# Another transfer model in the simulation that orders an attention and MoE kernel, new wanted times, and a column of ones written ahead of v's load

## The chip, the cores and the metric

The kernel runs on one core of one Trainium2 chip. The metric is the device time of one execution in microseconds (us), median of the runs shown.

## The reference

Queries are averaged in pairs along the sequence, attention is computed for 32 heads (4 batches of 8, 1152 keys, 576 pooled queries, 64 wide), and the result goes as 2304 tokens of 512 through one layer of products (512 to 1024 and back) with SoLU and a norm between them:

```python
q_pool = q.reshape(B, H, S // 2, 2, D).mean(axis=3)
scores = 1 / sqrt(D) * q_pool @ k.T
attn = exp(scores - max);  attn = attn / (sum + 1e-9)
x = (attn @ v)                      # to B * S/2 tokens of H * D = 512
h = x @ w_in                        # 512 -> 1024
e = exp(h - max);  solu = h * e / (sum(e) + 1e-9)
ln = (solu - mean) / sqrt(var + 1e-6) * g_ln
out = ln @ w_out                    # 1024 -> 512
```

## The kernel before

**Tiles and stages.** Heads are prepared in pairs: q, k and v are loaded, transposed on TensorE and split into a high and a low part, so that products keep float32 accuracy (`prep_k`, `prep_q2`, `add_v`). The low and high halves of k reach their places by four transfers from buffer to buffer (`k_put`), the two halves of q by four more (`q_beside`), and a second copy of k's high half by one (`k_again`). For each head `maxima` multiplies q by k once to find the row maxima. `scores` then takes nine steps a head (one for every 128 keys, 288 in all): products on TensorE, exponentials on ScalarE (once to float32 and once to float16, or float32 alone, from which VectorE casts where `use_dve` says so), the rest e - float16(e) on GpSimd (`rest`), and the products with v in groups of steps (`values`, grouped by `GR`). The first pair (18 steps) keeps float32 values in the buffer `vx`: there v lies in rows of 65 elements, the 65th a one that sums the weights. The weights of the two layers come in as 16 raw parts of 512 KB (`weight_part`), each turned into float32 by two ScalarE operations, one on GpSimd, two on VectorE, and split by one more on ScalarE and VectorE. Tokens go through the layers in 18 tiles (`tokens`). The last five need the last batch and run after the last step.

**Order.** Nothing here is put in order by hand. Every operation is given to a `Plan` with its engine, its length, what it reads and writes, and a wanted time `at`, counted in steps of the scores. `Plan.run` simulates the engines: of the operations that are ready it takes the one with the earliest wanted time on each engine, none that is wanted later than the current step plus a window (`win`), and it fills TensorE's idle time at the start with throw-away transposes (line 1374). The order in which the simulation starts operations is the order in which they are issued, engine by engine, and no engine passes over an instruction that waits. All transfers go by one queue, SP's. In the simulation a transfer takes SP for some time a call, enters one common line of transfers, and has an end that its readers wait for:

```python
if e == "SP":
    busy[e] = t + 670 * o.calls
    dma = max(dma, t + 1100) + length
    o.end = dma + 1000
```

**Names that the steps below use.** `KP` (line 21) holds all wanted times: `W` when the weight parts come, `M` when the tokens come, `P` when a pair's k, q and v are loaded and prepared, `N` and `N1` when the maxima start, `OF` other distances, `CD` which steps VectorE casts, `TP` up to which step the two halves of a step share one exponential of 576, `TX` up to which step a second pair of PSUM banks is used, `VM` which engines scale v of each pair, `GG` the head from which values are grouped in three instead of five groups. `v32` makes the buffer `vx`, `load_v32` loads the first pair's v into it, one head a call, and `add_v` sets the column of ones there by a memset on GpSimd (line 813).

Of the kernel before, what the change touches and what calls it, by code (L numbers as in the profile page):

```python
# [17 lines left out]
ALU = mybir.AluOpType  # L18
AXX = mybir.AxisListType.X

KP = {'W': [2, 4, 5], 'step': 0.5, 'M': [77, 15.3, 7.49], 'TX': 113, 'TP': 72, 'win': 5.01, 'P': [22.92, 18.98, 13.92, 23.51, 26.08, 30.44], 'N': [13, 7], 'AV': 3.97, 'CD': [73, 13], 'VM': 'BCCCCABCBABBCCAC', 'AH': 8, 'OF': [5.14, 2.07, 10.29, 1.04, 2.66], 'N1': 10.46, 'warm': 1, 'ws': 1.3, 'GR': 1, 'GG': 12, 'b_eh': 6, 'b_w1': 4, 'V0': -53.76, 'VF': 1, 'QD': [0, 1], 'L0': 0.97, 'F': 18}
FIRST = KP.get("L0", 0.3)


# [15 lines left out]
class Plan:  # L40
# [61 lines left out]
    def run(self):  # L102
# [16 lines left out]
        busy = dict.fromkeys(ready, 0)  # L119
# [65 lines left out]
        while events:  # L185
            t, what, _, arg = heapq.heappop(events)
            if what == 0:
                o, done = arg, done + 1
                for b in o.uses:
                    count[b] -= 1  # L190
                    for i in where[b]:
                        last[i][o.engine] = o
                    if not count[b]:
                        for i in where[b]:
                            held[i] = None
                        for e in ready:
                            push(t, 1, e)
                for m in after[o]:
                    e = m.engine
                    hop = self.HOP[o.engine][e] + (self.LOAD[m.kind] if e == "PE" != o.engine else 0)  # L200
                    if o.engine == e and not m.deps[o]:
                        hop = 0
                    m.ok_at = max(m.ok_at, t + hop)
                    m.left -= 1
                    if not m.left:
                        ready[e].append(m)
                        push(m.ok_at, 1, e)
                continue
            e = arg
            if busy[e] > t:  # L210
                continue
            best = None
            limit = 1e9 if not todo else now_mark + (self.window if todo < len(marks) else FIRST)
            for o in ready[e]:
                if o.at > limit or o.ok_at > t or (best is not None and (o.at, o.n) >= (best.at, best.n)):
                    continue
                g = buffers(o)
                if g is None:
                    continue
                s = could(o, g)  # L220
                if s > t:
                    push(s, 1, e)
                    continue
                best, got = o, g
            if best is None:
                if e == "PE" and self.warm and t > KP.get("ws", 2.5) * 1000 and todo > self.warm_until:
                    i = next((i for i in range(8) if held.get(i) is None), None)
                    if i is not None:
                        extra.append((t, lambda i=i: self.warm(i)))
                        busy[e] = t + (110 if t > self.COLD else 216)  # L230
                        push(busy[e], 1, e)
                continue
            o = best
            ready[e].remove(o)
            for b, c in got.items():
                where[b] = c
                before[b] = [x for i in c for x in last[i].values()]
                for i in c:
                    held[i] = b
                    last[i] = {}  # L240
                if b[0] in self.banks:
                    self.bank[b] = c
                else:
                    turn[self.tags[b[0]][0]] += 1
                head[b[0]] += 1
            for d in (*o.deps, *(x for b in o.uses for x in before.get(b, ()))):
                known[e][d.engine] = max(known[e][d.engine], d.rank)
            o.start, o.rank = t, ranks[e]
            ranks[e] += 1
            length = o.length  # L250
            if e == "PE":
                length += self.SWITCH if kind == "half" != o.kind else 0
                kind = o.kind
                length *= 1 if t > self.COLD else 2
            if e == "SP":
                busy[e] = t + 670 * o.calls
                dma = max(dma, t + 1100) + length
                o.end = dma + 1000
            else:
                busy[e] = o.end = t + length  # L260
            if o.mark is not None:
                todo -= 1
                if o.mark > now_mark or not todo:
                    now_mark = o.mark
            for x in ready:
                push(t, 1, x)
            push(o.end, 0, o)
            push(busy[e], 1, e)
# [25 lines left out]
    return 1.885 * n + 148  # L294


def DMA(n, fast=1):
    return n / (360 if fast else 180)


@with_exitstack
def attention_solu_moe(
# [10 lines left out]
    nc = tc.nc  # L313
# [146 lines left out]
    def weight_part(n, at, src, i, f, dst_h, dst_l, dst):  # L460
# [15 lines left out]
            else:  # L476
                nc.sync.dma_start(out=raw, in_=src[rows, c])

        add("SP", DMA(4096 * 128), at - 3, fetch, [], [("raw", n)])
        if wide:  # L480


# [59 lines left out]
    def pair(P, at_k, at_q, at_v, loads):  # L542
# [23 lines left out]
        def load_v32(i):  # L566
            nc.sync.dma_start(out=v32(P)[:, i, :, 0:D], in_=v[b, h0 + i].rearrange("(p j) d -> p j d", j=NJ))
# [7 lines left out]
        kb = 128 * NJ * D * 4  # L575
        KT = ("vx", 0, "kt") if P == FN == 1 else ("kt", P)
        if P:
            add("SP", DMA(2 * kb, 0), at_lk, load_k, [("vx", 0, 0, "one")] if P == FN == 1 else [], [KT], calls=2)
        else:
            add("SP", DMA(kb), at_lk, lambda: load_k0(0), [], [("kt", 0, 0)])  # L580
        add("SP", DMA(2 * kb), at_lq, load_q, [], [("qt", P, i) for i in range(3)])
        if not P:
            add("SP", DMA(kb), at_lk + 0.1, lambda: load_k0(1), [], [("kt", 0, 1)])
        if P < FN:
            for i in range(2):
                add("SP", DMA(kb, 0), at_lv + i / 10, lambda i=i: load_v32(i), [], [("vx", 0, P % 2, "v", i)])
        else:
            add("SP", DMA(2 * kb), at_lv, load_v, [], [("vt", P)])

# [43 lines left out]
        def k_put(h, lo):  # L633
            g = 2 * P + h
            if ("w1", g) not in tl:
                new(("w1", g), [128, S], FR)
            src = flat(tl["klo" if lo else "khi", P][D * h:D * h + D])
            dst = tl["w1", g][D * lo:D * lo + D, :]
            nc.sync.dma_start(out=dst.bitcast(F32), in_=src.bitcast(F32))
# [21 lines left out]
        def prep_k(i, at):  # L661
            ps, hi, lo = ("kps", (P, i)), ("khi", P, i), ("klo", P, i)
            add("PE", TR(3), at, lambda: k_tr(i), [KT], [ps], also=[hi, lo], kind="whole")
            add("ACT", ACT(PW), at, lambda: k_hi(i), [ps], [hi])
            add("DVE", DVE(PW) + 4, at, lambda: k_lo(i), [ps, hi], [lo])
            if i == 2:
                for h in range(2):
                    for l in range(2):
                        add("SP", DMA(64 * S * 4), at + 4 * h + 0.5, lambda h=h, l=l: k_put(h, l),
                            [("klo" if l else "khi", P)], [("w1", 2 * P + h, l)])  # L670

        def q_tr(i):
# [63 lines left out]
        def prep_q2(at):  # L736
            for i in range(2):
                ps, a = ("qps", (P, i)), at + 2 * i
                add("PE", TR(3 - i), a, lambda i=i: q_tr2(i), [("qt", P, 0)], [ps], also=[("q1", P), ("q2", P)], kind="whole")
                for odd in range(2):  # L740
                    n, o = ((384, 384), (256, 128))[i][odd], a + odd / 10
                    hi, lo = ("q1", P, i, odd), ("q2", P, 2 * i + odd)
                    add("ACT", ACT(n), o, lambda i=i, odd=odd: q_hi2(i, odd), [ps], [hi])
                    add("DVE", DVE(n), o, lambda i=i, odd=odd: q_lo2(i, odd), [ps, hi], [lo])
            for odd in range(2):
                add("SP", DMA(64 * 4 * 576, 0), at + 3, lambda odd=odd: q_beside(odd),
                    [("q1", P, i, odd) for i in range(2)], [("q1", P, 2, odd)], calls=2)
            add("SP", DMA(128 * 256, 0), at + 3, q_half, [("q1", P, 1, 0)], [("zq", P)], calls=2)

        for i in range(3):  # L750
            prep_k(i, at_k[i]) if P else prep_k0(i, 0, at_k[i], [])
# [57 lines left out]

        def add_v(after):  # L810
            if P < FN:
                if P < 2:
                    add("POOL", 160, -13, lambda: nc.gpsimd.memset(v32(P)[:, :, :, D:D + 1], 1.0),
                        [], [("vx", 0, P % 2, "one")])
                return
            V, S, H_ = ("vt", P), ("vs", P, 1), ("vhi", P, 0)
            add("ACT", ACT(2 * SQ, 1, 1), at_v, v_sum, [V, *after], [("am", P, 0), ("vlo", P, 0)])
# [135 lines left out]
    def scores(g, at):  # L953
# [8 lines left out]
        def k_again():  # L962
            nc.sync.dma_start(out=w2[g % 2][0:D, :].bitcast(F32), in_=tl["w1", g][0:D, :].bitcast(F32))

        add("SP", DMA(64 * S * 4), at - OF[0], k_again, [("w1", g)], [("w2", g)])

        def product(j, f):
            if NJ * g + j < TP:
# [345 lines left out]
    with tc.manual_schedule():  # L1314
# [46 lines left out]
        t = MS  # L1361
# [44 lines left out]
```

## Time and profile before

| | |
|---|---|
| median of 3 runs | 729.42 us (728.45 to 732.87) |
| the profiled execution | 732.07 us |
| its span, first to last instruction | 730.3 us |
| mean granted TensorE clock | 0.978 |
| TensorE, matmuls busy | 686.0 us, 94% of the span |
| ScalarE / VectorE / GpSimd busy | 534.7 / 506.5 / 486.4 us |
| the chain that ended last, by engine | TensorE 66%, VectorE 12%, ScalarE 8%, GpSimd 5%, transfers 3%, issue 5% |

The span is that of the profiled execution, and 1.8 us lie around it. A matmul's end is modelled, so a TensorE that counts as busy may still be held up. Idle time of an engine that doesn't set the end costs nothing. PE is TensorE's matmuls, PEld its weight loads, DVE VectorE, ACT ScalarE, POOL GpSimd, and SPq the transfers that SP issues.

### The profile page before, as it was taken

To read this page: it belongs to the slowest core of one execution; us is meant where nothing else is said; L and a number is where in the kernel's file an instruction comes from. 1 tells how busy PE (TensorE), PEld (TensorE's weight loads), DVE (VectorE), ACT (ScalarE), POOL (GpSimd) and SP (SyncE) were. 2 spreads that over 40 slices of the span, in tenths; PEclk is the share of its full clock that TensorE was granted. 3 is DMA by queue.
4 is the path that set the end of the run, shared out by engine and by line. 5 is a ranking of instruction groups with operands and counts; after the bars stand their busy time and mean duration, and the time that the engine had idled before them with its cause. 6 is when DMAs were issued, how large, how long until landed. Compare 5 with 4: busy or idle time off the path is not lost.

```text
span 730.3 us, 18791 instructions
## 1 busy us (share of the span) xinstructions
PE 686.0 (94%) x7048; PEld 598.7 (82%) x7048; DVE 506.5 (69%) x1221; ACT 534.7 (73%) x1327; POOL 486.4 (67%) x635
## 2 busy tenths in 40 slices
PE   7999787999989999999998999899999999999996
PEld 7989676777877888887887898788888898887885
DVE  5896786787887677877858684858586867425542
ACT  2656797989797687888778796778788877773432
POOL 1233796989788678697868677686967777681111
PEclk8999898999999999999999999999999999999999
DMA  8585566674453352536253434425445310000011
GB/s 206 156 210 152 152 161 160 180 182 101 123 120 96 90 135 53 133 88 163 41 128 98 113 84 113 101 65 135 101 102 130 91 42 18 17 16 22 15 30 29
DMA packets 78086, 75.79 MB, mean 104 GB/s; under 512 B 61108, under 2 KB 61228, under 8 KB 77996
## 3 DMA queue, kind: packets, MB, share of 16 engines
q1 hardware_dynamic: 77996, 74.60, 42.0%
q8 instruction: 55, 0.90, 0.5%
q14 instruction: 35, 0.29, 0.1%
HBM read 37.22 MB, written 4.72 MB: 57 GB/s over the span
## 4 chain that ended last, share of the span: by engine, by line
PE 66%; DVE 12%; ACT 8%; issue 5%; POOL 5%; DMA 3%; SPq 1%; ACTq 0%; DVEq 0%; POOLq 0%
PE bank L419 60%; DVE mx L859 4%; POOL eh L1005 3%; PE bank L1224 2%; ACT e L982 2%; PE bank L624 1%; ACT eh L988 1%; DVE q L422 1%; DVE eh L995 1%; DMA raw<-in_moe_w_in_dram 1%; PE bank L1374 1%; ACT e L988 1%; ACT q L718 1%; ACT eh L982 1%; DMA q<-q 1%
## 5 line engine op out<-in xcount | busy, mean ns | idle before, releaser
L1005 POOL TENSOR_TENSOR eh<-e,eh 128x64 f16<-128x64 f32 (+1 forms) x486 | 381.2, 809 | 123.7 <-ACT e L982 29.1
L859 DVE TENSOR_REDUCE mx<-bank 128x1 f32<-128x384 f32 x420 | 220.5, 550 | 79.4 <-PE bank L419 76.5
L419 PE MATMUL bank<-q,w 128*128 128x288 f32 (+1 forms) x1152 | 242.6, 314 | 11.3 <-ACT e L982 7.9
L419 PEld LDWEIGHTS bank<-q,w 128*128 128x128 f32 (+1 forms) x1152 | 188.2, 192 | 37.1 <-ACT e L982 17.8
L982 ACT ACTIVATE eh<-bank 128x288 f16<-128x288 f32 x376 | 159.1, 425 | 59.4 <-PE bank L419 57.2
L982 ACT ACTIVATE e<-bank 128x288 f32<-128x288 f32 x432 | 180.8, 427 | 22.5 <-POOL eh L1005 10.8
L419 PE MATMUL bank<-w,q 128*128 128x384 f32 x390 | 133.9, 371 | 12.9 <-DVE q L422 5.4
L419 PEld LDWEIGHTS <-eh 128*128 128x128 f16 x3834 | 126.6, 99 | 18.4 <-issue 11.2
L419 PE MATMUL bank<-vhi,eh 128*128 128x65 f16 x2484 | 136.2, 196 | 1.8 <-POOL eh L1005 0.9
L419 PE MATMUL bank<-vlo,eh 128*128 128x64 f16 x1350 | 133.1, 194 | 0.0
L419 PEld LDWEIGHTS bank<-w,q 128*128 128x128 f32 x390 | 72.8, 194 | 26.8 <-DVE mx L859 7.8
L1207 POOL TENSOR_TENSOR st<-st 128x1 f32<-128x1 f32 x54 | 23.4, 432 | 57.0 <-ACT junk L1194 53.9
L988 ACT ACTIVATE eh<-bank 128x576 f16<-128x576 f32 (+1 forms) x72 | 47.6, 667 | 12.6 <-PE bank L419 12.0
L493 POOL TENSOR_TENSOR up<-up,un 128x512 f32<-128x512 f32 x16 | 20.9, 1309 | 32.2 <-ACT un L486 14.9
L1155 DVE TENSOR_REDUCE st<-bank 128x1 f32<-128x512 f32 x36 | 24.7, 686 | 24.4 <-PE bank L419 24.3
L422 DVE TENSOR_TENSOR q<-bank,q 64x384 fp32r<-64x384 f32 (+2 forms) x63 | 28.8, 458 | 16.4 <-ACT q L718 13.4
L419 PE MATMUL bank<-woh,lh 128*128 128x512 f32 x104 | 34.3, 416 | 3.2 <-DVE e L1174 3.1
L988 ACT ACTIVATE e<-bank 128x576 f32<-128x576 f32 x54 | 36.1, 672 | 0.2 <-POOL eh L1005 0.2
L419 PE MATMUL bank<-wih,xl 128*128 128x512 f32 x104 | 33.8, 409 | 0.0
L419 PE MATMUL bank<-wol,lh 128*128 128x512 f32 x104 | 32.9, 399 | 0.0
L419 PE MATMUL bank<-wih,xh 128*128 128x512 f32 x104 | 32.7, 403 | 0.0
L419 PE MATMUL bank<-wil,xh 128*128 128x512 f32 x104 | 32.7, 398 | 0.0
(134 smaller groups left out, 1064.9 us busy)
## 6 DMA issues: line engine op xcount, KB each, us to landing
qt<-in_q_dram SPq DMA_DIRECT2D x16, 576.0 KB
w<-w SPq DMA_DIRECT2D x32, 288.0 KB
kt<-in_k_dram SPq DMA_DIRECT2D x30, 288.0 KB
vt<-in_v_dram SPq DMA_DIRECT2D x15, 576.0 KB
w<-khi SPq DMA_DIRECT2D x30, 288.0 KB
w<-klo SPq DMA_DIRECT2D x30, 288.0 KB
out_dram<-o SPq DMA_DIRECT2D x36, 128.0 KB
raw<-in_moe_w_in_dram SPq DMA_DIRECT2D x8, 511.6 KB
```

The lines of the kernel that those rows point to most:

```text
L419: nc.tensor.matmul(out=o, lhsT=a, rhs=b, start=first, stop=last, skip_group_check=True)
L422: nc.vector.tensor_tensor(out=o, in0=a, in1=b, op=ALU.subtract)
L493: nc.gpsimd.tensor_tensor(out=up, in0=up, in1=tl["un", n].bitcast(F32), op=ALU.subtract)
L624: nc.tensor.transpose(ps[:, c, :], tl["kt", P][:, 3 * i + c].rearrange("p h d -> p (h d)"), ident)
L718: nc.scalar.copy(out=tl["q1", P][r, :, t, :], in_=ps)
L859: nc.vector.tensor_reduce(out=tl["mx", g][:, m, c:c + 1], in_=tl["nps", (g, m, c)], op=ALU.max, axis=AXX)
L982: nc.scalar.activation(out=tl[name, (g, j)][:, f * HALF:(f + 1) * HALF], in_=tl[tn(j, f), (g, j, f)], func=ACTF.Exp, scale=ESC,)
L988: nc.scalar.activation(out=new((name, (g, j)), [128, SQ * 4 // mybir.dt.size(dtype)], dtype)[:, 0:SQ].rearrange("p (f i) -> p f i", f=2), ...
L1005: nc.gpsimd.tensor_tensor(out=e[:, o:o + c.stop - c.start], in0=e32[:, c], in1=e[:, c], op=ALU.subtract)
L1155: nc.vector.tensor_reduce(out=st(f), in_=tl[H_[f]], op=ALU.max, axis=AXX)
L1207: nc.gpsimd.tensor_tensor(out=st(o), in0=st(a), in1=nhalf if b is None else st(b), op=op)
L1224: nc.tensor.transpose(ps[:, c, :], tl[E][:, o:o + 128], ident)
```

## The change

The simulation's transfers change in three places: an SP call takes 640 ns instead of 670, a transfer enters the line after 1200 ns instead of 1100, and its end is 2000 ns (`DL`) instead of 1000 after its last byte. Its bytes per ns are no longer 360 or 180 but 300, 260, 250 or 200 by kind. The wanted times in `KP` are other ones. The memset of the ones is put ahead of v's load: it is wanted at -40 instead of -13, and the load names the column as something that it reads, so that it is simulated and issued after the memset. Which instructions exist changes only by `CD`, `TP`, `VM` and `GG`.

```diff
-KP = {'W': [2, 4, 5], 'step': 0.5, 'M': [77, 15.3, 7.49], 'TX': 113, 'TP': 72, 'win': 5.01, 'P': [22.92, 18.98, 13.92, 23.51, 26.08, 30.44], 'N': [13, 7], 'AV': 3.97, 'CD': [73, 13], 'VM': 'BCCCCABCBABBCCAC', 'AH': 8, 'OF': [5.14, 2.07, 10.29, 1.04, 2.66], 'N1': 10.46, 'warm': 1, 'ws': 1.3, 'GR': 1, 'GG': 12, 'b_eh': 6, 'b_w1': 4, 'V0': -53.76, 'VF': 1, 'QD': [0, 1], 'L0': 0.97, 'F': 18}
+KP = {'W': [2.0, 3.15, 5], 'step': 0.46, 'M': [77, 16.35, 7.49], 'TX': 114, 'TP': 76, 'win': 4.7, 'P': [22.28, 18.98, 13.92, 24.38, 26.08, 32.99], 'N': [12.95, 7], 'AV': 4.32, 'CD': [65, 16], 'VM': 'BCCCCABCBAACCCAC', 'AH': 8, 'OF': [6.79, 2.07, 11.42, 1.2, 1.48], 'N1': 9.3, 'warm': 1, 'ws': 1.3, 'GR': 1, 'GG': 6, 'b_eh': 6, 'b_w1': 4, 'V0': -60.99, 'VF': 1, 'QD': [0, 1], 'L0': 0.97, 'F': 18, 'DL': 2000}
...
-                busy[e] = t + 670 * o.calls
-                dma = max(dma, t + 1100) + length
-                o.end = dma + 1000
+                busy[e] = t + 640 * o.calls
+                dma = max(dma, t + 1200) + length
+                o.end = dma + KP.get("DL", 1000)
...
-def DMA(n, fast=1):
-    return n / (360 if fast else 180)
+def DMA(n, rate=300):
+    return n / rate
...
-        add("SP", DMA(4096 * 128), at - 3, fetch, [], [("raw", n)])
+        add("SP", DMA(4096 * 128, 250), at - 3, fetch, [], [("raw", n)])
...
-        add("SP", DMA(2 * kb), at_lq, load_q, [], [("qt", P, i) for i in range(3)])
+        add("SP", DMA(2 * kb, 260), at_lq, load_q, [], [("qt", P, i) for i in range(3)])
...
         if P < FN:
+            if P < 2:
+                add("POOL", 160, -40, lambda: nc.gpsimd.memset(v32(P)[:, :, :, D:D + 1], 1.0),
+                    [], [("vx", 0, P % 2, "one")])
             for i in range(2):
-                add("SP", DMA(kb, 0), at_lv + i / 10, lambda i=i: load_v32(i), [], [("vx", 0, P % 2, "v", i)])
+                add("SP", DMA(kb, 200), at_lv + i / 10, lambda i=i: load_v32(i), [("vx", 0, P % 2, "one")],
+                    [("vx", 0, P % 2, "v", i)])
...
-                        add("SP", DMA(64 * S * 4), at + 4 * h + 0.5, lambda h=h, l=l: k_put(h, l),
+                        add("SP", DMA(64 * S * 4, 200), at + 4 * h + 0.5, lambda h=h, l=l: k_put(h, l),
...
-                add("SP", DMA(64 * 4 * 576, 0), at + 3, lambda odd=odd: q_beside(odd),
+                add("SP", DMA(64 * 4 * 576, 200), at + 3, lambda odd=odd: q_beside(odd),
...
         def add_v(after):
             if P < FN:
-                if P < 2:
-                    add("POOL", 160, -13, lambda: nc.gpsimd.memset(v32(P)[:, :, :, D:D + 1], 1.0),
-                        [], [("vx", 0, P % 2, "one")])
                 return
...
-        add("SP", DMA(64 * S * 4), at - OF[0], k_again, [("w1", g)], [("w2", g)])
+        add("SP", DMA(64 * S * 4, 200), at - OF[0], k_again, [("w1", g)], [("w2", g)])
```

The loads of k, the second half of the q copies and the 16 KB copies (`q_half`) go to 200 as well, which is left out here.

## Rows read from the trace of the kernel before

**Rows 1.** The page: busy us, share of the span, instructions.
```profile
PE 686.0 (94%) x7048; PEld 598.7 (82%) x7048; DVE 506.5 (69%) x1221; ACT 534.7 (73%) x1327; POOL 486.4 (67%) x635
```

**Rows 2.** The waits: us in total, times, longest us.
```profile
PEld L419 <- issue: 11.2, 43, 0.7
...
PE bank L419 <- ACT e L982: 7.9, 16, 1.8
```

**Rows 3.** The timeline's start: us, duration, what, [idle before, releaser].
```profile
0.72 0.39 SPq L561 DMA_DIRECT2D qt<-in_q_dram  x1
...
2.10 6.14 SPq L567 DMA_DIRECT2D vx<-in_v_dram  x2
...
4.74 0.63 DVE L593 TENSOR_TENSOR qt<-qt 128x192 f32<-128x192 f32 x2 [1.50 <-DMA qt<-in_q_dram]
4.79 1.28 ACT L597 ACT_TABLE_LOAD   x1 [4.79 <-DMA qt<-in_q_dram]
...
7.53 0.13 POOL L813 MEMSET vx<- 128x18 f32 x1 [5.37 <-DMA vx<-in_v_dram]
7.60 0.59 POOL L593 TENSOR_TENSOR qt<-qt 128x192 f32<-128x192 f32 x1
8.22 0.35 ACT L597 COPY qt<-qt 128x192 f32<-128x192 f32 x1 [2.15 <-POOL qt L593]
...
8.48 1.22 ACT L649 CAST w<-bank 64x384 fp32r<-64x384 f32 x3
...
9.58 0.90 PE L675 MATMUL bank<-ident,qt 128*128 128x128 f32 x3 [2.80 <-DVE w L422]
```

**Rows 4.** The chain of waits from 60 to 80 us: start, us, what.
```profile
65.43 1.40 SPq L639
...
66.87 7.26 DMA raw<-in_moe_w_in_dram
```

**Rows 5.** The timeline from 60 to 80 us.
```profile
74.16 0.75 ACT L486 ACTIVATE up<-raw,ebias 128x512 int32<-128x512 int8 x1 [5.08 <-DMA raw<-in_moe_w_in_dram]
...
75.34 0.64 ACT L718 CAST q<-bank 64x256 fp32r<-64x256 f32 x2
...
76.79 1.28 PE L419 MATMUL bank<-w,q 128*128 128x384 f32 x2 [4.07 <-DVE q L422]
```

**Rows 6.** The timeline from 96 to 124 us.
```profile
106.02 3.25 SPq L728 DMA_DIRECT2D q<-q  x4
...
113.69 0.66 PE L419 MATMUL bank<-w,q 128*128 128x384 f32 x1 [4.42 <-DMA q<-q]
```

**Rows 7.** The timeline around 457 us.
```profile
456.54 0.59 ACT L1230 CAST lh<-bank 128x512 fp32r<-128x512 f32 x1 [2.26 <-DMA out_dram<-o]
...
457.80 0.54 PE L419 MATMUL bank<-q,w 128*128 128x288 f32 x2 [1.79 <-ACT e L982]
```

**Rows 8.** Busy time by window: length, PE, PEld, DVE, ACT, POOL; PEclk, DMA share, GB/s.
```profile
30.00:40.00 10.00, 10.00 (x83) 9.72 (x82) 9.06 (x20) 8.20 (x16) 1.83 (x2) 1.00 0.87 234
...
40.00:50.00 10.00, 9.54 (x56) 7.24 (x56) 9.83 (x22) 4.00 (x7) 5.62 (x4) 1.00 1.06 209
75.00:85.00 10.00, 7.99 (x53) 6.61 (x53) 7.69 (x16) 8.11 (x15) 8.13 (x6) 0.66 0.33 94
110.00:120.00 10.00, 6.31 (x89) 6.00 (x90) 5.02 (x14) 4.98 (x9) 4.10 (x4) 0.66 0.75 192
140.00:150.00 10.00, 8.05 (x86) 6.56 (x82) 8.51 (x22) 9.78 (x19) 9.53 (x9) 0.91 0.98 238
455.00:465.00 10.00, 8.01 (x72) 6.65 (x71) 6.16 (x19) 5.17 (x14) 4.28 (x6) 0.83 0.39 94
```

**Rows 9.** Groups by line and shape: busy us, mean ns of one, idle before.
```profile
L982 ACT ACTIVATE e<-bank 128x288 f32<-128x288 f32 x432 | 180.8, 427 | 22.5 <-POOL eh L1005 10.8 <-PE bank L419 10.7
...
L988 ACT ACTIVATE e<-bank 128x576 f32<-128x576 f32 x54 | 36.1, 672 | 0.2 <-POOL eh L1005 0.2
...
L995 DVE CAST eh<-e 128x576 f16<-128x576 f32 x28 | 17.4, 623 | 14.9 <-ACT e L982 14.6
...
L497 DVE TENSOR_SCALAR bank<-raw 128x512 int32<-128x512 int32 x16 | 10.9, 683 | 0.1
```

More of the change, by code (lines that the diff above doesn't have):

```diff
@@ L577, in pair @@
         if P:
-            add("SP", DMA(2 * kb, 0), at_lk, load_k, [("vx", 0, 0, "one")] if P == FN == 1 else [], [KT], calls=2)
+            add("SP", DMA(2 * kb, 200), at_lk, load_k, [("vx", 0, 0, "one")] if P == FN == 1 else [], [KT], calls=2)
         else:
             add("SP", DMA(kb), at_lk, lambda: load_k0(0), [], [("kt", 0, 0)])
-        add("SP", DMA(2 * kb), at_lq, load_q, [], [("qt", P, i) for i in range(3)])
+        add("SP", DMA(2 * kb, 260), at_lq, load_q, [], [("qt", P, i) for i in range(3)])
         if not P:
@@ L745, in prep_q2 @@
             for odd in range(2):
-                add("SP", DMA(64 * 4 * 576, 0), at + 3, lambda odd=odd: q_beside(odd),
+                add("SP", DMA(64 * 4 * 576, 200), at + 3, lambda odd=odd: q_beside(odd),
                     [("q1", P, i, odd) for i in range(2)], [("q1", P, 2, odd)], calls=2)
-            add("SP", DMA(128 * 256, 0), at + 3, q_half, [("q1", P, 1, 0)], [("zq", P)], calls=2)
+            add("SP", DMA(128 * 256, 200), at + 3, q_half, [("q1", P, 1, 0)], [("zq", P)], calls=2)
         for i in range(3):
```

## The prediction

> **What bounds the kernel now.** I read the page first. TensorE's matmuls are busy for 686.0 us, far ahead of the other engines [rows 1], so 44 us (730.3 less 686.0) is all the idle time that an order can give back, with whatever the clock costs on top. I then went through TensorE's timeline for every idle stretch of 0.45 us or more: 24 of them, 28.8 us together. Four end on something that a transfer held up, and they make 13.1 us: 2.80 at 9.58 us [rows 3], 4.07 at 76.79 us [rows 5], 4.42 at 113.69 us [rows 6] and 1.79 at 457.80 us [rows 7]. The other twenty share 15.8 us, mostly below a microsecond each.
>
> Last came the windows, for what the clock and the other engines do there. The clock reads 0.66 in the ten microseconds round the second stall, 0.66 round the third and 0.83 round the fourth: between its levels of 1.2 and 2.4 GHz, after TensorE had stood still. From 40 to 50 us VectorE is busy for 9.83 of 10 us, and TensorE, which counts as busy for 9.54, gets only 56 matmuls through; in the ten microseconds before there were 83 [rows 8]. So that stretch is VectorE's, whatever the busy share says.
>
> **The column of ones.** Its memset stands behind v's load in the program, and both touch the interleaved rows of `vx`. The row shows what comes of it: the memset sits idle on GpSimd for 5.37 us until the load is in, runs for 0.13 us, and only then may GpSimd add the last third of q, which ScalarE copies at 8.22 us and behind which its first cast of k stands at 8.48 us. The second call of v's load is stuck behind the memset too (two calls take SP 6.14 us) [rows 3].
>
> Put first, the memset costs 0.13 us in a stretch in which GpSimd waits for q anyway. q is in by 4.74 us, as VectorE's own part of the addition starts then. GpSimd's addition (0.59 us) would end at about 5.35. ScalarE loads its table until 4.79 + 1.28 = 6.07, copies for 0.35, and casts k from about 6.4 us: 2.1 us earlier. The transposes of q at 9.58 wait for the banks of those casts, and everything to the first maxima follows. SP gains 5.4 us for what is queued behind v's second call: the first weight part, k of the second pair and the first copy of k. What is lost: v's load, issued at 2.10, waits for the memset, 0.3 us at most, and v is first read behind the first exponentials. I take **-2.1 us**. Bounds: 0, if the throw-away transposes or VectorE's reductions fill the gap, and -2.8, the whole of TensorE's wait [rows 3].
>
> **The transfer model.** At 66.87 us the chain waits 7.26 us for a weight part that was issued right behind four copies of k [rows 4]. The old model gives 1.1 us, 524 KB / 360 and 1.0 us: 3.6 us, with a line that is soon empty. In the new one the four copies take 1.47 us each in line, so that the part, entering at about 69.6, has its last byte at 71.7 and ends at 73.7; ScalarE got it at 74.16 [rows 5]. The copies of q issued from 106.02 us are alike: alone in line the old model ends them at 110.3 us (the second call pair 1.34 us later, 1.1, 147 KB / 180, 1.0), and TensorE got them at 113.69 [rows 6]. So the new numbers are right where the old ones let an engine run into a wait.
>
> In a quiet line it is otherwise. q's 590 KB were issued at 0.72 and used at 4.74 us, 4.0 us [rows 3]; the old model gives 3.7 and the new one 5.5. The Trainium skill ("DMA: Bandwidth & Descriptors", Anatomy of one DMA) fits a transfer by a fixed 2.0 us and its bytes at 436 GB/s, for the gpsimd queue. By that a weight part alone would take an estimated 3.2 us, and the old model would be the better one; the 7.26 us in this trace are more than twice that, behind other copies.
>
> What a right model can give back is bounded by the three later stalls, 4.07 + 4.42 + 1.79 = 10.3 us, and by the clock that they cost: 7.99 x 0.34 + 6.31 x 0.34 + 8.01 x 0.17 = 6.2 us [rows 5 to 8]. At the second stall there was work to put ahead: the casts of q that TensorE needed stood on ScalarE behind the weight part, ready, and ran at 75.34 as soon as it was in [rows 5]. At the third TensorE itself is first in line for the copies, and other products can go ahead only as far as exponentials are there. So I take half of both: **-5.1** and **-3.1 us** (each between nothing and the whole).
>
> **Weights earlier.** The first eight parts are wanted 3.15 instead of 4 steps apart, the last one at 62.2 instead of 69. That pulls about one more part into the stretch round 40 to 50 us, which is VectorE's: three operations of 0.68 us [rows 9], **+2.1 us** (0 to +4.1, for two). It takes one out of the stretch from 140 to 150 us, where ScalarE is busy for 9.78 of 10 us and TensorE idles for 1.95 [rows 8]: **-1.0 us** (0 to -2.0).
>
> **Fewer instructions.** `CD` gives 35 instead of 28 steps whose float16 VectorE casts: ScalarE loses seven times two exponentials of 0.427 us, 6.0 us, and VectorE gains 7 x 0.62 = 4.4 us. `TP` joins four more steps: 4 x (4 x 0.427 - 2 x 0.672) = 1.5 us off ScalarE [rows 9]. `VM` moves the scaling of two pairs from ScalarE to VectorE, an operation each. Of TensorE's waits 7.9 us end on these exponentials [rows 2], and ScalarE's total falls by under 2%: **-1.0 us** (+2 if VectorE becomes late by it, to -3). `GG` takes two of five groups of value products from each of six heads: 12 fewer changes of kind. The weight loads have 43 gaps of 0.26 us there, but they mostly lie under running matmuls [rows 2]: **-0.5 us** (0 to -3.1). `V0` and the first letter of `VM` reach nothing, as the first pair returns before it uses them.
>
> **The rest of the new order.** Window, loads of v and k, distances of the tokens and the lag of the maxima all move, and the trace of before can't show where they end. The nearest rows are the twenty small stalls of 15.8 us. An order that is dealt anew drops some and makes others; I take **+2.0 us**, between -4 and +6.
>
> Sum: -2.1 - 5.1 - 3.1 + 2.1 - 1.0 - 1.0 - 0.5 + 2.0 = **-8.7 us**. Against the profiled execution, 732.07 us, that is 723.4; it stood 2.65 us above the median, so against 729.42 I forecast **720.7 us**, 1.2% faster.
>
> **The rivals.**
> 1. *The stalls only change their names.* A reader that is planned later still leaves TensorE without other work, or the caution of 1.5 us in a quiet line costs what it saves in a full one. For it: at 113.69 us TensorE, not a neighbour, waits for the copies. Against: the casts at 75.34 were ready. The start alone is left, with half a microsecond for the groups: 729.42 - 2.6 = 726.8 us. By the page's fit the old model would be right, and this would be the result.
> 2. *Everything goes.* All of the three stalls and their clock, 16.5 us, and the start, 2.1 us, go, and the small gains of 2.5 only pay for the weights (+2.1): 729.42 - 18.6 - 0.4 = 710.4 us; with the +2.0 of the new order 712.4.
> 3. *Slower: weight parts meet a full line.* From 40 to 50 us the transfers are already at a share of 1.06 [rows 8]. One more part there lands late, ScalarE stands behind it as at 74.16, and TensorE and its clock follow: 4.07 + 2.7 = 6.8 us each. It decides from two such stalls on in place of the one that is there, with none of the others cured and two parts more in VectorE's stretch: 729.42 - 2.1 + 6.8 + 4.1 = 738.2 us. Against it: the new model has these parts in line, so it would have to be wrong by microseconds again.
>
> **How the numbers follow.** The forecast has 0.60, rival 1 has 0.22, rival 2 has 0.10, rival 3 has 0.08. A measurement of this kernel tells about 1%, 7.3 us, from no change: 722.1 and 736.7 are the borders. Of the forecast's spread (712 to 728, from the halves that I took) 0.42 lies below 722.1 and 0.18 above. With rival 2 and 0.03 of rival 1 faster has 0.55; same has 0.18 + 0.18 = 0.36; slower has 0.09, with 0.01 of rival 1. Rival 1 belongs in the range with some 3 us above it, and the range goes down to the first case of rival 2; rival 3, half of rival 2 and the far ends of the others, 0.2 together, are left out: **711 to 730 us**.
>
> **What the profile of after would show.** Right: the memset near 2.2 us without a wait, ScalarE's first cast of k near 6.4 us and the first transposes of q near 7.5; no stall of TensorE above 2 us that ends on a transfer, or on something that waited for one; no ScalarE row of several microseconds' wait for a weight part; a granted clock of 1.00 in the windows that read 0.66. Wrong: such stalls of 3 us or more in other places between 40 and 160 us (rivals 1 and 3); fewer matmuls than 56 from 40 to 50 us; or a start that saves less than 1 us because the transposes that keep TensorE's clock up are planned for longer than they are needed.

## The result and the profile after

The changed kernel takes 706.1 us in the median of 4 runs (704.49 to 707.55) beside 729.97 us for the kernel before: a ratio of 0.9668, with a 95% interval of 0.9626 to 0.971. It is 3.3% faster; I had forecast 1.2%, and 706.1 lies under the range of 711 to 730. The profiled execution took 707.54 us, with a span of 705.8 us and a mean granted clock of 0.990. One execution of a variant below (old_end) took 1281.72 us, where its three others took 706.44 to 706.78; it is in no interval and moves that median from 706.64 to 706.71.

First the page and the waits, to set beside [rows 1, 2].

```profile
PE 677.7 (96%) x7060; PEld 596.5 (85%) x7060; DVE 518.8 (74%) x1230; ACT 528.6 (75%) x1305; POOL 486.4 (69%) x634
```

```profile
PEld L419 <- issue: 5.7, 24, 0.4
PE bank L419 <- ACT e L983: 5.7, 15, 0.7
```

TensorE's idle time fell from 44 us to 28 us (705.8 less 677.7), and its busy time fell too, by 8 us, although it has 12 instructions more. These twelve are throw-away transposes, 87 instead of 75; the section on the change had named only `CD`, `TP`, `VM` and `GG` for what exists. TensorE's own timeline shows where. Before, 24 idle stretches of 0.45 us or more made 28.8 us; now there are 16, and they make 11.0 us. Behind the first instruction these are the two longest of them, where [rows 5 to 7] have 4.07, 4.42 and 1.79:

```profile
35.01 0.44 PE L419 MATMUL bank<-w,q 128*128 128x384 f32 x1 [0.94 <-DVE q L422]
...
89.98 0.80 PE L419 MATMUL bank<-q,w 128*128 128x288 f32 x4 [0.94 <-ACT e L989]
```

The start, beside [rows 3]: the memset (now line 586) waits for nothing, GpSimd and ScalarE go on as soon as q is in, and the transposes of q run at 6.15 us instead of 9.58.

```profile
1.98 0.20 POOL L586 MEMSET vx<- 128x18 f32 x1
...
2.21 1.88 SPq L567 DMA_DIRECT2D vx<-in_v_dram  x2
...
4.49 1.28 ACT L601 ACT_TABLE_LOAD   x1 [4.49 <-DMA qt<-in_q_dram]
4.50 0.76 POOL L597 TENSOR_TENSOR qt<-qt 128x192 f32<-128x192 f32 x1 [2.31 <-DMA qt<-in_q_dram]
...
5.79 0.35 ACT L601 COPY qt<-qt 128x192 f32<-128x192 f32 x1
...
6.15 0.62 PE L679 MATMUL bank<-ident,qt 128*128 128x128 f32 x3
...
7.18 0.85 ACT L653 CAST w<-bank 64x384 fp32r<-64x384 f32 x2
```

The windows, beside [rows 8]:

```profile
30.00:40.00 10.00, 9.06 (x66) 8.82 (x65) 8.07 (x17) 7.01 (x13) 3.29 (x3) 0.86 0.67 146
40.00:50.00 10.00, 9.99 (x35) 8.33 (x36) 7.37 (x18) 1.40 (x2) 4.06 (x3) 0.50 1.04 253
75.00:85.00 10.00, 9.43 (x154) 8.16 (x152) 9.11 (x19) 9.62 (x17) 8.89 (x8) 1.00 0.83 220
110.00:120.00 10.00, 9.58 (x127) 8.08 (x123) 7.94 (x18) 10.00 (x18) 10.00 (x8) 1.00 0.93 252
140.00:150.00 10.00, 9.19 (x129) 8.14 (x128) 8.59 (x18) 9.87 (x17) 9.54 (x8) 1.00 0.98 248
455.00:465.00 10.00, 9.73 (x94) 8.69 (x93) 5.33 (x16) 8.44 (x25) 8.81 (x14) 1.00 0.02 4
```

The clock stands at 1.00 in the three windows that read 0.66, 0.66 and 0.83. From 40 to 50 us, on the other hand, only 35 matmuls pass instead of 56, at a clock of 0.50, with VectorE busy for 7.37 us.

**Where the time came from.** I cut both traces at the same points of the work: the end of head 0's first score product, of head 11's first, and of the last one. This is the kernel before, by windows, and under it the changed one.

```profile
24.18:227.43 203.25, 184.69 (x2034) 162.58 (x2034) 160.38 (x356) 167.71 (x348) 146.34 (x138) 0.96 0.60 150
227.43:654.03 426.60, 412.06 (x4523) 360.54 (x4523) 297.04 (x755) 334.67 (x915) 323.15 (x454) 0.99 0.38 91
654.03:730.30 76.27, 69.79 (x370) 56.85 (x369) 34.44 (x79) 27.00 (x55) 13.26 (x28) 0.99 0.10 23
```

```profile
20.36:213.45 193.09, 182.41 (x2044) 161.87 (x2044) 160.85 (x358) 165.66 (x338) 145.67 (x137) 0.96 0.66 160
213.45:623.72 410.27, 400.81 (x4488) 355.19 (x4487) 304.65 (x757) 327.62 (x898) 321.52 (x449) 1.00 0.40 92
623.72:705.80 82.08, 75.70 (x396) 61.25 (x395) 38.08 (x86) 29.90 (x60) 15.38 (x33) 1.00 0.11 25
```

The start gives 3.8 us (24.18 to 20.36), heads 0 to 10 give 10.2 (203.25 to 193.09), heads 11 to 31 give 16.3 (426.60 to 410.27), and the tail takes 5.8 back (76.27 to 82.08), as 26 matmuls have moved into it. Together that is 24.5 us, the whole difference of the spans. I had looked for most of the gain in the first two parts.

### The profile page after: what moved, and what is told of

It reads as the page before. It is cut to its first block, busy times and chain, and to the rows that moved or that the text cites. A ratio compares the mean times of both kernels' runs of the same rounds, so it can differ in the third digit from the quotient of the medians.

```text
span 705.8 us, 18795 instructions
## 1 busy us (share of the span) xinstructions
PE 677.7 (96%) x7060; PEld 596.5 (85%) x7060; DVE 518.8 (74%) x1230; ACT 528.6 (75%) x1305; POOL 486.4 (69%) x634
## 4 chain that ended last, share of the span: by engine, by line
PE 68%; DVE 14%; ACT 9%; POOL 5%; issue 3%; DVEq 0%; POOLq 0%; ACTq 0%
PE bank L419 59%; DVE mx L860 5%; POOL eh L1006 3%; PE bank L1225 2%; PE bank L628 2%; PE bank L1375 2%; ACT e L983 1%; POOL st L1208 1%; ACT e L989 1%; DVE e L1212 1%; ACT eh L989 1%; DVE st L1156 1%; PE bank L712 1%; ACT q L722 1%; PE bank L1136 1%
## 5 line engine op out<-in xcount | busy, mean ns | idle before, releaser
L419 PE MATMUL bank<-q,w 128*128 128x288 f32 (+1 forms) x1152 | 237.3, 310 | 9.9 <-ACT e L983 5.7
L983 ACT ACTIVATE e<-bank 128x288 f32<-128x288 f32 x424 | 175.5, 429 | 33.0 <-POOL eh L1006 20.7
L983 ACT ACTIVATE eh<-bank 128x288 f16<-128x288 f32 x358 | 149.9, 429 | 37.5 <-PE bank L419 35.3
L419 PE MATMUL bank<-w,q 128*128 128x384 f32 x390 | 131.8, 366 | 3.3 <-DVE q L422 1.6
L419 PEld LDWEIGHTS <-eh 128*128 128x128 f16 x3834 | 122.4, 98 | 12.8 <-issue 5.7
L419 PE MATMUL bank<-vhi,eh 128*128 128x65 f16 x2484 | 130.8, 194 | 1.4 <-POOL eh L1006 0.7
L419 PE MATMUL bank<-vlo,eh 128*128 128x64 f16 x1350 | 128.4, 193 | 0.0
L1208 POOL TENSOR_TENSOR st<-st 128x1 f32<-128x1 f32 x54 | 25.4, 470 | 57.1 <-ACT junk L1195 55.4
L493 POOL TENSOR_TENSOR up<-up,un 128x512 f32<-128x512 f32 x16 | 20.5, 1280 | 35.7 <-ACT up L486 13.3
L989 ACT ACTIVATE e<-bank 128x576 f32<-128x576 f32 x58 | 39.4, 682 | 2.0 <-POOL eh L1006 1.1
L422 DVE TENSOR_TENSOR q<-bank,q 64x384 fp32r<-64x384 f32 (+2 forms) x63 | 28.8, 458 | 10.2 <-ACT q L722 7.3
L419 PE MATMUL bank<-woh,ll 128*128 128x512 f32 x104 | 32.8, 404 | 0.0
```

What stands on the lines that cost most here:

```text
L419: nc.tensor.matmul(out=o, lhsT=a, rhs=b, start=first, stop=last, skip_group_check=True)
L422: nc.vector.tensor_tensor(out=o, in0=a, in1=b, op=ALU.subtract)
L493: nc.gpsimd.tensor_tensor(out=up, in0=up, in1=tl["un", n].bitcast(F32), op=ALU.subtract)
L983: nc.scalar.activation(out=tl[name, (g, j)][:, f * HALF:(f + 1) * HALF], in_=tl[tn(j, f), (g, j, f)], func=ACTF.Exp, scale=ESC,)
L989: nc.scalar.activation(out=new((name, (g, j)), [128, SQ * 4 // mybir.dt.size(dtype)], dtype)[:, 0:SQ].rearrange("p (f i) -> p f i", f=2), ...
L1208: nc.gpsimd.tensor_tensor(out=st(o), in0=st(a), in1=nhalf if b is None else st(b), op=op)
```

## The experiments

Each was timed beside the kernel before on one chip, but not all on the same one: the kernel before has medians from 728.07 to 730.13 us there, and the changed kernel was timed once. Where the intervals of two kernels overlap, I don't tell them apart. The stages are those of the cut above, in the profiled execution of each; "later" is heads 11 to 31 with the tail. Times are medians. Diffs of `KP` show the changed entries alone.

| kernel | us | ratio to before, 95% | start | heads 0 to 10 | later |
|---|---|---|---|---|---|
| before | 729.97 | | 24.2 | 203.3 | 502.9 |
| changed | 706.10 | 0.9626 to 0.9710 | 20.4 | 193.1 | 492.4 |
| ones_first | 725.77 | 0.9923 to 0.9991 | 19.7 | 203.9 | 500.3 |
| ones_behind | 707.59 | 0.9688 to 0.9784 | 21.9 | 191.0 | 492.3 |
| new_model | 721.56 | 0.9831 to 0.9943 | 20.5 | 203.0 | 497.3 |
| old_model | 720.13 | 0.9812 to 0.9922 | 19.3 | 204.4 | 490.8 |
| times_only | 721.80 | 0.9839 to 0.9939 | 23.2 | 206.8 | 490.7 |
| old_end | 706.71 | 0.9678 to 0.9740 | 19.8 | 194.1 | 491.0 |
| old_rates | 705.51 | 0.9634 to 0.9741 | 19.9 | 193.9 | 490.4 |
| old_weights | 712.70 | 0.9722 to 0.9799 | 21.1 | 197.7 | 492.6 |
| model_weights | 718.79 | 0.9847 to 0.9901 | 20.8 | 198.2 | 498.1 |
| old_pairs | 711.29 | 0.9720 to 0.9778 | 20.2 | 199.6 | 489.8 |
| old_window | 710.34 | 0.9701 to 0.9790 | 19.8 | 194.6 | 492.3 |
| old_rest | 716.15 | 0.9812 to 0.9866 | 20.6 | 201.1 | 492.8 |
| early_only | 714.61 | 0.9779 to 0.9849 | 19.9 | 192.2 | 500.6 |
| mix_only | 723.91 | 0.9895 to 0.9960 | 23.2 | 202.3 | 495.4 |
| old_mix | 708.50 | 0.9655 to 0.9741 | 20.4 | 195.3 | 491.4 |
| old_tokens | 710.68 | 0.9678 to 0.9788 | 20.6 | 193.5 | 494.5 |
| old_values | 708.44 | 0.9667 to 0.9752 | 20.6 | 194.7 | 492.8 |
| old_mix_tokens | 709.10 | 0.9701 to 0.9790 | 20.2 | 192.8 | 494.5 |

### The column of ones

**ones_first**: the kernel before, with the two lines of the memset moved ahead of v's load as in the change.

> The kernel before with only the memset of the ones put ahead of v's load (old transfer model, old wanted times). The start of the changed kernel has head 0's first score product at 20.36 us instead of 24.18. If the start is worth that in full, the time is 3 to 4 us under the kernel before, about 726 us (my forecast's term said 2.1). If the time saved at the start is eaten by the weight part that ScalarE waits for near 70 us, it is the same as before, 729 to 731 us.

**ones_behind**: the changed kernel, with them moved back.

```diff
-            if P < 2:
-                add("POOL", 160, -40, lambda: nc.gpsimd.memset(v32(P)[:, :, :, D:D + 1], 1.0), ...
...
         def add_v(after):
             if P < FN:
+                if P < 2:
+                    add("POOL", 160, -13, lambda: nc.gpsimd.memset(v32(P)[:, :, :, D:D + 1], 1.0), ...
```

> The changed kernel with the memset of the ones behind v's load as before. The start's price: 709 to 711 us (3.3 us measured on the kernel before, 3.8 us between the traces at the first score product). If the changed order hides the start behind the slow stretch from 35 to 50 us: 705 to 707 us.

Alone it takes the time from 729.12 to 725.77 us on that chip, and the timeline of ones_first has the two rows that I had named, 6.4 and 7.5 us:

```profile
6.40 1.21 ACT L653 CAST w<-bank 64x384 fp32r<-64x384 f32 x3
...
7.51 0.55 PE L679 MATMUL bank<-ident,qt 128*128 128x128 f32 x3 [0.65 <-DVE w L422]
```

Head 0's first product ends 4.5 us earlier, more than the 2.1 that were summed up. The rest is the clock: TensorE no longer stands for 2.80 us, and from 10 to 15 us the clock reads 1.00 in ones_first and 0.50 in the kernel before. The windows have that stretch so, first in ones_first and then in the kernel before:

```profile
10.00:15.00 5.00, 5.00 (x39) 4.54 (x38) 5.00 (x12) 0.00 (x0) 0.00 (x0) 1.00 1.19 207
```

```profile
10.00:15.00 5.00, 5.00 (x23) 4.90 (x21) 3.37 (x7) 1.44 (x3) 0.00 (x0) 0.50 1.15 272
```

In the changed kernel the same edit costs 1.5 us when it is undone (707.59), which this measurement can't tell from nothing. In the traces its start comes 1.5 us later and heads 0 to 10 take 2.1 us less. That is the clock and not the order, for the two kernels issue the same instructions in the same order on every engine. TensorE's timeline of the changed kernel, and then that of ones_behind:

```profile
35.56 7.20 PE L419 MATMUL bank<-vx,eh 128*128 128x65 f32 x40
42.52 2.93 PE L419 MATMUL bank<-w,q 128*128 128x384 f32 x6
...
59.35 2.34 PE L419 MATMUL bank<-vx,eh 128*128 128x65 f32 x20
```

```profile
36.53 0.44 PE L419 MATMUL bank<-w,q 128*128 128x384 f32 x1 [0.94 <-DVE q L422]
...
37.07 4.58 PE L419 MATMUL bank<-vx,eh 128*128 128x65 f32 x40
41.45 2.64 PE L419 MATMUL bank<-w,q 128*128 128x384 f32 x6
...
57.70 2.34 PE L419 MATMUL bank<-vx,eh 128*128 128x65 f32 x20
```

ones_behind is 1.5 us behind at the forty value products, and 1.7 us ahead 22 us later: its clock is 1.00 in these products and 0.83 from 40 to 50 us, where the changed kernel's is 0.50. So some 3 us between two traces in heads 0 to 10 need no cause in the order.

### The transfer model

**new_model**: the changed kernel with the whole table of before.

```diff
-KP = {'W': [2.0, 3.15, 5], ... 'F': 18, 'DL': 2000}
+KP = {'W': [2, 4, 5], ... 'F': 18, 'DL': 2000}
```

> The changed kernel with the wanted times, window and instruction mix of before: what remains is the new transfer model and the memset. Theory M (the model brings the gain, since its ends of transfers are right): the stalls that a transfer held up are gone, and the time is 706 to 714 us. Theory T (the wanted times bring it): the start and a part of the three stalls are gone, and the time is 719 to 727 us.

**old_model**: the changed kernel with the model of before. **old_end** has the first three lines of its edit alone, **old_rates** the last alone.

```diff
-                busy[e] = t + 640 * o.calls
-                dma = max(dma, t + 1200) + length
-                o.end = dma + KP.get("DL", 1000)        # DL 2000
+                busy[e] = t + 670 * o.calls
+                dma = max(dma, t + 1100) + length
+                o.end = dma + KP.get("DL", 1000)        # DL 1000
...
-    return n / rate
+    return n / {300: 360, 260: 360, 250: 360, 200: 180}[rate]    # copies of k: 360
```

> The changed kernel with the transfer model of before (670 and 1100 ns, 1000 ns to the end, 360 or 180 bytes per ns); new wanted times, mix and the memset stay. Theory M: stalls of 2 us and more on transfers come back, and the time is 716 to 726 us. Theory T: 705 to 712 us.

> The changed kernel with the new rates of bytes, but the fixed times of before (670 and 1100 ns, and 1000 ns to the end). The whole model undone cost 14 us. If the end that lies 1 us too early is what lets engines run into transfers, most of it is lost here: 715 to 720 us. If it is the rates, that is the queue behind other transfers, 706 to 710 us.

> The changed kernel with the rates of before (360 and 180 bytes per ns), and the new fixed times with the end 2000 ns after the last byte. The fixed times undone alone cost 0.6 us. If the rates carry the model's 14 us: 716 to 721 us, lost before head 11. If each of the two halves is enough: 705 to 709 us.

**times_only**: the kernel before with the new table, without `DL`.

> The kernel before with only the table of wanted times replaced (with the mix in it); old transfer model, memset behind v's load. Theory M: 722 to 731 us, as the old model lets engines run into transfers. Theory T: 3 to 4 us above the changed kernel for the start, 708 to 715 us.

Both theories fall. ones_first, which has the start, gives 3.3 us, the model 4.2 more, the times alone 7.3, and all of it together 23.9: 9 us come only of model and times together. The table says why. What lies behind head 11 comes with the times, whatever the model (490.7 and 490.8 with the old one, 492.4 with the new). What lies in heads 0 to 10 comes from neither: 203.0 with the model alone, 206.8 with the times alone, 193.1 with both. And no one number of the model carries it. With its fixed times undone it is 706.71 us, with its rates undone 705.51: neither can be told from the changed kernel, and only both together cost 14 us. old_end fell into the range that I had given to the rates as the cause, which old_rates then refutes; old_rates fell into the range for "each of the two halves is enough". Either half makes transfers end later in the simulation than the old model does, and an order made with either is as fast.

With the model alone the three stalls of before are gone, as forecast, but a new one stands in their place. This is the timeline of new_model, the queue of transfers and then TensorE:

```profile
41.88 3.28 SPq L732 DMA_DIRECT2D q<-q  x4
...
47.98 2.00 PE L419 MATMUL bank<-w,q 128*128 128x384 f32 x4 [8.82 <-DMA q<-q]
```

The copies of q for the second pair are issued at 41.88 us (in the changed kernel at 32.38), behind loads of k and q for the third pair and weight parts, and TensorE stands for 8.82 us. The old model under the new times has smaller ones, in the timeline of old_model:

```profile
51.11 0.80 PE L419 MATMUL bank<-q,w 128*128 128x288 f32 x4 [3.16 <-ACT eh L989]
...
146.54 0.62 PE L419 MATMUL bank<-w,q 128*128 128x384 f32 x2 [1.72 <-DMA zq<-q]
```

### Heads 0 to 10: which times the model needs

**old_weights**: the changed kernel with

```diff
-'W': [2.0, 3.15, 5], 'step': 0.46
+'W': [2, 4, 5], 'step': 0.5
```

> The changed kernel with the weight parts wanted as before (4 steps apart instead of 3.15 for the first eight, step 0.5). My forecast had the earlier parts cost 1.1 us net, so 704 to 706 us if that is right. If they take ScalarE's load out of the stretch from 80 to 180 us, it loses 3 to 6 us there: 709 to 712 us.

**model_weights**: new_model with that edit the other way round.

> New transfer model and memset with the wanted times of before (721.6 us so far), and of the new ones only the weight parts' (3.15 apart, step 0.46). With the old spacing a weight part stands among the copies of k near 29 us, ScalarE waits for it before it casts q, and TensorE stalls for 8.8 us at 48 us on the copies of q; the changed kernel has the part at 27.1 us, ahead of the copies. If that is the whole interaction, the stall goes and the time is 710 to 715 us. If each pairing of model and times is a deal of its own, it is 717 to 725 us.

**old_rest**: the changed kernel with `OF`, `AV`, `win`, `N`, `N1`, `P` and `TX` of before.

> The changed kernel with the remaining wanted times of before (OF, AV, window, N, N1, P, TX); model, memset, weight parts, tokens and mix are new. If the named parts carry the gain, 706 to 710 us. If the remaining times carry what is not yet placed after head 11 (some 5 us), 711 to 716 us.

**old_pairs**: the changed kernel with

```diff
-'P': [22.28, 18.98, 13.92, 24.38, 26.08, 32.99], 'N': [12.95, 7], 'N1': 9.3
+'P': [22.92, 18.98, 13.92, 23.51, 26.08, 30.44], 'N': [13, 7], 'N1': 10.46
```

> The changed kernel with P, N and N1 of before (when a pair's k and v are loaded and prepared, when the maxima start). If these bring head 1 through the stretch from 35 to 50 us, the stall of 8 us on the copies of q near 48 us is back and most of the 10 us are lost: 712 to 717 us. If not: 705 to 709 us.

**old_window**: the changed kernel with `'win': 5.01`.

> The changed kernel with the window of before, 5.01 instead of 4.7 steps. If the window carries the 10 us: 712 to 717 us. If not, and the order is dealt a little anew: 705 to 709 us.

Undoing the weights' spacing costs 6.6 us and undoing the pairs' times 5.2 (4.6 and 6.5 in the traces' heads 0 to 10), and each brings the same wait back. The timelines of old_weights and old_pairs:

```profile
39.65 2.72 SPq L732 DMA_DIRECT2D q<-q  x4
...
46.04 2.92 PE L419 MATMUL bank<-w,q 128*128 128x384 f32 x6 [6.58 <-DMA q<-q]
```

```profile
40.52 3.85 SPq L732 DMA_DIRECT2D q<-q  x4
...
50.35 2.00 PE L419 MATMUL bank<-w,q 128*128 128x384 f32 x4 [11.31 <-DMA q<-q]
```

What the edits have in common shows in the queue of transfers. Neither is about the second pair's own copies of q: `P` holds the times of the pairs from the third on, and `W` those of the weight parts. But both decide what stands ahead of these copies. In the changed kernel the copies go first, and the load of the third pair's k comes behind them; in old_pairs that load goes first:

```profile
32.38 2.86 SPq L732 DMA_DIRECT2D q<-q  x4
...
41.28 3.57 SPq L553 DMA_DIRECT2D kt<-in_k_dram  x2
```

```profile
31.32 3.35 SPq L553 DMA_DIRECT2D kt<-in_k_dram  x2
```

So it is in all twenty traces: TensorE stands for 5 us or more somewhere between 38 and 51 us in the six that have the third pair's k and q both ahead (new_model, old_weights, model_weights, old_pairs, old_rest and old_end, with the copies issued from 37.9 to 42.0 us), and in no other (copies from 31.3 to 36.3 us). Which of `P`, `N` and `N1` turns the order in old_pairs was not separated. model_weights, with the model and the spacing but the old preparation, still stalls for 8.34 us near 48 us (the profile puts the end of this wait down to VectorE's work on a weight part): my story that the spacing alone removes it was wrong.

The length of the wait is not its price, though. old_end has it too, and can't be told from the changed kernel; this is its timeline:

```profile
43.23 2.92 PE L419 MATMUL bank<-w,q 128*128 128x384 f32 x6 [5.01 <-DMA q<-q]
```

Before that wait it runs the same forty value products in 4.58 us that took 7.20 in the changed kernel's execution. The window alone shifts the time by 4.2 us, to between my two ranges; its interval overlaps that of the changed kernel (0.9701 to 0.979 beside 0.9626 to 0.971), so I read nothing into it.

### After head 11

**mix_only**: the kernel before with the first edit below; **old_mix**: the changed kernel with it reversed; **old_tokens**: the changed kernel with the second; **old_values**: with the third; **old_mix_tokens**: with the first reversed and the second; **early_only**: with all three (the first reversed) and `'TX': 113`.

```diff
-'CD': [73, 13], 'TP': 72, 'VM': 'BCCCCABCBABBCCAC', 'GG': 12
+'CD': [65, 16], 'TP': 76, 'VM': 'BCCCCABCBAACCCAC', 'GG': 6
...
-'M': [77, 16.35, 7.49]
+'M': [77, 15.3, 7.49]
...
-'OF': [6.79, 2.07, 11.42, 1.2, 1.48], 'AV': 4.32
+'OF': [5.14, 2.07, 10.29, 1.04, 2.66], 'AV': 3.97
```

> The kernel before with only CD, TP, VM and GG of the changed one; transfer model, memset and wanted times of before. Theory X: 717 to 721 us. Theory Y: 727 to 731 us.

> The changed kernel with CD, TP, VM and GG of before (28 casts by VectorE instead of 35, and so on); model, memset and all other wanted times stay. From head 11 to the last step the changed kernel gains 16.3 us on the kernel before, whatever the transfer model (17.9 with the old one), and gives back about 6 after it. Theory X (the mix frees ScalarE, which brings these 11 us): 715 to 719 us, with the loss between head 11 and the last step. Theory Y (the tokens' spacing and other wanted times bring them): 705 to 710 us.

> The changed kernel with the tokens wanted 15.3 instead of 16.35 steps apart; all else stays. Theory Y (the spacing brings the 11 us after head 11): 713 to 719 us. Theory X: 705 to 709 us, with the last step some 5 us later and a tail that is as much shorter.

> The changed kernel with OF and AV of before (second copies of k 5.14 instead of 6.79 steps ahead, value products 3.97 instead of 4.32 steps behind, the tokens' distances). If these carry the 10 us: 712 to 717 us, lost before head 11. If not: 705 to 709 us.

> The changed kernel with both the mix (CD, TP, VM, GG) and the tokens' spacing of before. If the two are what acts after head 11 and add up: 712 to 715 us, with heads 0 to 11 as in the changed kernel. If they stand in for one another: 716 to 719 us. If neither matters but the deal: 706 to 710 us.

> The changed kernel with mix, tokens, OF, AV and TX of before: new are the model, the memset, the weight parts, P, N, N1 and the window, that is what was found to act before head 11. If the early part stands by itself, head 11 is 12 to 14 us ahead of the kernel before and the time is 714 to 718 us. If it needs the other wanted times as well, a stall of several microseconds near 45 us is back and the time is 718 to 723 us.

How far these stages can be read shows in a pair that stands already in the table: ones_first issues the same instructions in the same order on every engine as the kernel before (only the memset's place among the transfers differs), and has 500.3 us later where that has 502.9. Its window from head 11 to the last step differs in the clock, 1.00 and 0.99, and in TensorE's busy time, 409.44 and 412.06 us. So 2.5 us there are no order's doing.

```profile
223.56:647.68 424.12, 409.44 (x4524) 358.52 (x4523) 296.77 (x755) 334.58 (x915) 322.71 (x454) 1.00 0.38 91
```

Against my ranges, mix_only and old_tokens fell between those of the two theories, old_mix_tokens fell into that of "neither matters but the deal", and early_only came as expected.

early_only keeps what acts early, and there it stands by itself: 192.2 us in heads 0 to 10, no more than in the changed kernel. Behind head 11 it has 500.6, as ones_first has. So these three edits (with `TX`, one step) carry the later gain, some 8 us (500.6 to 492.4). Two other orders without them, new_model and model_weights, have 497.3 and 498.1 there, so it can be as little as 5. The three don't add up, though. The mix gives 4.9 us there over ones_first (500.3 to 495.4) and takes nothing when it is undone (491.4, and 494.5 with or without it under the old tokens). `OF` and `AV` take nothing either (492.8), but with mix and tokens undone, they (with `TX`) are worth 6 us (494.5 to 500.6). By these totals the mix and these distances stand in for one another; the tokens' spacing has 2 us on top, within what the clock alone can do to a trace. Undone, it costs 4.6 us in the medians, with intervals that overlap.

The stage rows of old_mix_tokens and early_only from head 11 to the last step, by windows:

```profile
213.00:630.70 417.70, 408.39 (x4524) 361.08 (x4524) 297.84 (x756) 334.75 (x914) 323.81 (x454) 1.00 0.38 91
```

```profile
212.09:636.43 424.34, 411.29 (x4523) 361.23 (x4523) 298.05 (x756) 334.06 (x915) 322.74 (x453) 0.99 0.38 90
```

Set beside the stage rows of before and after: under the old spacing TensorE has the same 4523 or 4524 matmuls to do before the last step, with the new one 4488, and the tail is longer by 5.8 us. The idle time up to there is 13.1 us in early_only, 9.3 in old_mix_tokens, 9.5 in the changed kernel and 14.5 before.

## Why the prediction was wrong

- **Direction: right. The cause of the early gain: right in part.** The four stalls are gone. But with the model's later ends alone (new_model) a new one came, and heads 0 to 10 take 203.0 us where ones_first has 203.9: the model gave that gain only together with the new times. Rival 2 ("everything goes", 710.4 to 712.4 us) was the nearest case, and I gave it 0.10.
- **The memset: right in mechanism, too small in size.** The two times that I named came out to 0.1 us in ones_first. The term of -2.1 us measured -3.3 alone, as the stall's clock, which I had counted for the other three, was left out for this one; that lies beyond the bound of -2.8 too.
- **The three stalls and their clock: too small.** "Half of both" had one row for it and one against, and none for its size. For heads 0 to 10 the forecast had half of the two stalls, -4.2, half of their clock, -2.4, and the weights, +1.1: -5.5 us. Measured: -10.2, and -12.2 in ones_behind's execution of the same order.
- **Weights earlier: wrong sign.** I charged +2.1 us for a part more in VectorE's stretch from 40 to 50 us. Undone, the spacing costs 6.6 us. That the stretch was VectorE's holds for the kernel before, whose chain of waits runs through it up to 48.36 us:

```profile
35.76 0.42 DVE q L422
...
43.51 1.93 DVE mx L859 x4
...
47.79 0.57 DVE mx L859
48.41 1.37 PE bank L419 x7
```

  In the changed kernel's execution VectorE has room there (7.37 of 10 us). What the term left out is the queue: with the old spacing the second pair's copies of q are issued at 39.65 us instead of 32.38, and TensorE waits for them for 6.58 us. The sign that I gave for a failure, fewer than 56 matmuls there, came true (35) beside a gain: the clock of that execution was 0.50 there. ones_behind has 46, at 0.83.
- **The step that failed most: "the rest of the new order", +2.0 us, between -4 and +6.** For all that lies behind head 11 the forecast had -1.6 for the fourth stall and its clock, -1.5 for the fewer instructions and +2.0: -1.1 us. Measured: -10.5, of which the clock alone may be 2.5. I had priced a new deal of the order by the small stalls that the list shows, as if it could only replace them. But TensorE's 97% there are not all work: of the 16.3 us up to the last step 5.1 are idle time, 5.9 have moved into the tail, and 5.3 more were counted as busy (412.06 - 400.81 - 5.9). 2.6 of these 5.3 can be the clock's, as ones_first has 409.44 for the same instructions. Why the rest counted as busy is not shown.
- **Fewer instructions: -1.5 us, an addition that can't be made.** The mix is worth 6.2 us alone; in company the medians differ by 2.4, with intervals that overlap.
- **Rivals 1 and 3: not seen here.** Rival 1's mechanism is real, as new_model shows: old stalls went and one of 8.82 us came, though even so it was 4.2 us under ones_first.

**What stays open.** Why either half of the model is enough was not traced to single instructions: old_rates has the copies of q first, as the changed kernel, and old_end has them last and loses only 1.0 us in heads 0 to 10 with its wait of 5.01. Why the old model under the new times loses 11.3 us there, with the waits of 3.16 and 1.72 us shown above, is open too. Every one of these orders is a deal of its own, and differences under some 3 us are not resolved between them; that the three later edits act through fewer waits of ScalarE and GpSimd, and not through the deal, is argued from the totals, not shown. No version beat the changed kernel: old_rates with 705.51 us can't be told from it.

## What to carry to other kernels

Where a planner sets the order, cost its change by stages cut at the same work, not by the list of stalls: here 24.5 us went, and all stalls of before that a transfer held up made 13.1. Read a stall's whole price, the engine's idle time and the clock after it. When a load moves in time, look at what it stands ahead of in its queue, and not only at the engine that will work on it. Two kernels with the same order show what the clock alone does to a stage: look for such a pair before reading small differences. Test parts in both directions: here the model gave 4 us without the new times and 14 with them.

## What the runs showed of the hardware

The clock fell without a long wait. In the changed kernel TensorE counts as busy from 35.01 to 50 us, and the idle stretch before that is 0.94 us. It had run 14 of forty float32 value products of 65 columns when the granted clock fell, at about 37.1 us, from 1.00 to 0.50, and it read 0.50 from 38 to 50 us. The forty, from 35.56 us, took 7.20 us (0.18 each); in ones_behind, behind the same instructions and an idle stretch of 0.94 us as well, they took 4.58 (0.11 each) at a clock of 1.00. So here neither the instructions nor the idle stretch before them told which clock was granted.

Copies from buffer to buffer took far longer in a full line than a load of twice the bytes did at the start. In old_pairs the copies of q, 288 KB in four calls, are issued from 40.52 us and reach TensorE at 50.35, 9.8 us later, with the transfers' share at 1.04 and 219 GB/s moved from 40 to 50 us. The first load of q, 576 KB, took 4.0 us [rows 3], with that share at 0.64 from 0 to 5 us.
